# Attention of the last three batches on four 64x64 quadrants of the array

## The chip, the cores and the metric

The kernel runs on one core of one Trainium2 chip. A core has five engines that work side by side: TensorE (PE in the profile, its weight loads PEld), VectorE (DVE), ScalarE (ACT), GpSimd (POOL) and SyncE (SP). PE multiplies a stationary operand, loaded ahead as weights, with a moving operand, and writes the result to PSUM. Its array has 128 rows and 128 columns; a matmul whose operands cover 64 rows and 64 columns uses one quadrant of it. The row half follows from the SBUF partitions of the operands (0 to 63 or 64 to 127), the column half from the PSUM partitions of the output. DMA transfers are issued by POOL (loads that convert float32 to bfloat16) and by SP (transposes between SBUF tiles, and the stores).

The metric is device time in microseconds, the median of several runs; less is better.

## The reference

Two stages. The first is attention with 8 batches, 8 heads, 576 tokens and head size 64. The lower four heads see a plain window of 32 tokens, the upper four a dilated one: 32 tokens, every fourth. The second is a feed-forward block with a squared ReLU, on 4608 tokens of 512 features and a hidden size of 2048.

```python
scores = scale * np.matmul(q, k.transpose(0, 1, 3, 2))
mask_plain = (rel >= 0) & (rel < window)
mask_dil = (rel >= 0) & (rel < window * dilation) & (rel % dilation == 0)
scores = np.where(masks[None, :, :, :], scores, -1000000000.0)
attn = np.exp(scores - np.max(scores, axis=-1, keepdims=True))
attn = attn / (np.sum(attn, axis=-1, keepdims=True) + 1e-09)
out = np.matmul(attn, v)
x = out.transpose(0, 2, 1, 3).reshape(B * S, H * D)
h = np.maximum(x @ w_in, 0.0)
result = h * h @ w_out
```

## The kernel before, in words

**Feed-forward.** Tokens come in tiles of 512 (the first 1024 tokens in tiles of 256). A tile of 512 is 32 groups of four matmuls of 512 columns: 16 groups of `mm1` (L683), each followed by a ReLU on ACT (L696) and a square on DVE (L697), and 16 groups of `g2` (L725); after every fourth of these, ACT copies the result out (L731) and SP stores it. Four PSUM buffers `pf` rotate. Groups are numbered through the kernel; group 128 starts tile 4.

**Attention.** Heads go in pairs `e` = 0 to 3; head 2e lies in partitions 0 to 63, head 2e+1 in 64 to 127. Pairs 0 and 1 are plain, 2 and 3 dilated; they are taken in the order 0, 2, 1, 3. Tokens stand by their residue modulo 4 (`r`, 4 of them) and then by `m` (144 of them). Keys come in nine blocks of 64. For a plain pair, block `i` meets 24 positions of each residue, so 96 queries; for a dilated one, a block of 64 positions of one residue meets 96 or 80 positions of the same residue. The ninth block, the remainder of 64 tokens, meets 64 queries.

For batches 1 to 7 a block's keys stand block-diagonally in `kbd` (128x128: one head's keys in each half, zeros elsewhere) and its values likewise in `vbd`, so that one matmul of the full array serves both heads. `scores` (L312, L318) makes half a pair at a time: matmuls into a PSUM buffer `pa`, Exp on ACT (L322), a mask product on DVE (L323). For batches from 3 on it also adds the overlapping parts of neighbouring blocks into `pm` (L332), so that the sums need to stream only 576 columns per pair and not one per block and query. `pv` (L422, L424) makes the products with the values in `po` and the sums, with a block of ones, in `pd`; then Ln and Exp(-x) on ACT (L426, L427) and a product on DVE (L437) write the normalised result into `xT`, which the feed-forward part reads. There are two `pa`, one `po` and one `pd`.

**Batch 0** has a path of its own (`first_step`). Its scores (L559) and some of its products (L597) use two diagonal quadrants of 64x64 at a time. Its transposes (L507) use column halves, and its warming matmuls (L477, `idle`) the whole array.

**Operands.** Q and K of a batch are loaded by POOL (`load_qk`, L161), transposed by SP into `xx` (`cross`, L216), and rearranged by DVE into `qT` and `kbd` (`halves`: L256 for Q, L260 for K of plain pairs, L267 and L273 for dilated ones), 16 copies for Q and 24 for K per batch. V is loaded by POOL (`load_v`: L178 plain, L191 dilated, L197 remainder); DVE spreads the dilated part into `vbd` (`spread_v`, L207).

**Order.** The schedule is written by hand. `PROGRAM` names what runs after each group up to 128: `5q0` is Q of pair 0 of batch 5, `4b3` the second half of the scores of pair 3 of batch 4, `4o1` and `4p1` the products of the first and the second half of pair 1, `L5:...` a load. Batches 5 to 7 follow from rules at the end of the kernel: for batch b, pair number x of the order gets its scores `a` and `b` at groups 32(b-1) + 8x - 2 and + 0, its products `o` and `p` at + 3 and + 6. Each engine takes its instructions in the order in which they are written; V of batch b is loaded from group 32(b-2) on, Q and K from 32(b-3) + 6, the transposes are written at 32(b-2) + 5.

Of the kernel before, what the change touches and what calls it, by code (L numbers as in the profile page):

```python
# [12 lines left out]
RES = 4  # L13
# [16 lines left out]
    "2k1h | 2q1 2k2 L3:x | | 2q2 2p0 L3:vwpdr 2a1 | | | 2b1 | 2o1 2a2 2v2 2q3 | | 2p1f | 2k3 | 2b2 2o2 | 2v3 | "  # L30
    "2a3 2p2f L4:q10123 | 2b3 2o3 | 3k1 | 2p3 | 3q1v L4:q00123 | 3k0l | | 3a1 3k0h | | 3k2l | 3o1 3q0a | 3k2h "
    "| | | 3a0 | 3b1 | 3q2 | | 3p1 L4:x L4:vwpdr | 3v2 | 3b0 | 3a2 3q3l 3o0 3q3h 3k3 | | | 3o2 3b2 | 4q1 | 3p0 "
    "3v3 | 3a3 | 3p2 4q2 4q0 | L5:q10123 3b3 4k0al | 3o3 4k0ah | 4k1 | | L5:q00123 3p3 4k2 4k3 4a0 L5:vwpdr | "
    "| | 4b0 | | 4q3 | | 4o0 | | | 4a2 4v2 | 4b2 | 4a3 L5:x 4a1 | 4o2 | | | 4p2 L6:q00123 4v3 | | 4b1 | | 4p0 "
    "| | 4p1 | 5q0 5k0 | 4b3 | | | | 4o1 | | 5k2 L6:q10123 4o3 | 5q2 5k1 | | 4p3 | 5q1 |"
)


# [25 lines left out]
def kernel(  # L64
# [9 lines left out]
    nc = tc.nc  # L74
# [21 lines left out]
    PARTED = (0, 1)  # L96
    STAGE = (0, 1, 0, 2, 2, 2, 0, 1)
    ADDED = 3
    RING = 4 * S
    KT = DM // P  # L100
    NF = DFF // P
# [35 lines left out]
    xx = [const.tile([P, 2, H * 2 * M], bf16, name=f"xx{i}") for i in range(2)]  # L137
    qx, kx = [[t[:, x, :].rearrange("p (h c m) -> p h c m", h=H, c=2) for t in xx] for x in range(2)]
    qk0 = xx[0][:, :, :].rearrange("p x (e r m) -> p x e r m", e=NE, r=RES)
    k8 = const.tile([P, NE // 2, 64], bf16, name="k8")  # L140
    idle = const.tile([P, 256], bf16, name="idle")
    kbd = const.tile([P, NE, NB, P], bf16, name="kbd")
    vbd = [const.tile([P, NE, NB, P], bf16, name=f"vbd{i}") for i in range(2)]

    mk_dram = nc.inline_tensor(_masks(), name="mask_patterns")

# [156 lines left out]
    def scores(b: int, e: int, part: int):  # L303
        ps = ps_a.tile([P, 512], f32, name="pa")
        if part == 0:
            pts[e] = p_pool.tile([P, NB * 96], bf16, name="pt")
        pt = pts[e]
        n = 0
        for i, r, m0, m1 in blocks(b, e, part):
# [40 lines left out]
    def pv(b: int, e: int, part: int, spare=None, name=""):  # L350
# [71 lines left out]
            nc.tensor.matmul(oo, vb[:, e, i, :], rh, start=(x == 0), stop=(x == len(mms) - 1), skip_group_check=True)  # L422
        for x, (dd, rh) in enumerate(dms):
            nc.tensor.matmul(dd, ones[:, :], rh, start=(x == 0), stop=(x == len(dms) - 1), skip_group_check=True)  # L424
        rec = r_pool.tile([P, 512], f32, name="rec")
        nc.scalar.activation(rec[:, 0:n], d[:, 0:n], ACT.Ln)  # L426
        nc.scalar.activation(rec[:, 0:n], rec[:, 0:n], ACT.Exp, scale=-1.0)  # L427
        t0 = b * S % RING
# [12 lines left out]
    def step(b: int, code: str):  # L441
# [19 lines left out]
        else:  # L461
            pv(b, e, part)

    first = {}
    held = []
    sides = [slice(64 * hl, 64 * hl + 64) for hl in range(2)]
# [14 lines left out]
    def first_step(code: str):  # L481
# [56 lines left out]
        elif what == "S":  # L538
# [2 lines left out]
                first["S", e, part] = pool.tile([P, 512], f32, name=nm)  # L541
            ps = first["S", e, part]
            if part == 0:
                pts[e] = p_pool.tile([P, NB * 96], bf16, name="pt")
            bl = blocks(0, e, part)
            y = 0
            for x, (i, r, q0, q1) in enumerate(bl):
# [62 lines left out]
        elif what == "D":  # L610
            dms = first.pop(("D", e, part))
            for x, (dd, rh) in enumerate(dms):
                nc.tensor.matmul(
                    dd, ones, rh, start=(x == 0 and y0 == 0), stop=(x == len(dms) - 1), skip_group_check=True
                )
        else:
            n = 512 if part == 0 else w
            if what == "L":
                first["X", e, part] = rec = r_pool.tile([P, 512], f32, name="rec")
                nc.scalar.activation(rec[:, 0:n], first["P", e, part][1][:, 0:n], ACT.Ln)  # L620
            elif what == "X":
                rec = first["X", e, part][:, 0:n]
                nc.scalar.activation(rec, rec, ACT.Exp, scale=-1.0)
            else:
                o, rec = first["P", e, part][0][:, 0:n], first.pop(("X", e, part))[:, 0:n]
                to = xT[:, e, RES * m0 : RES * m0 + n]
                if part == 0:
                    to = xT[:, e : e + 2, 0:w]
                    o, rec = [x.rearrange("p (e n) -> p e n", e=2) for x in (o, rec)]
                nc.vector.tensor_tensor(out=to, in0=o, in1=rec, op=ALU.mult)  # L630
# [172 lines left out]
    def run(code):  # L803
# [21 lines left out]
        elif code[0] in "wW":  # L825
            n, _, at = code[1:].partition("+")
            turn(int(n), 512 if code[0] == "w" else 256, [int(x) for x in at])
        elif code[0] in "TCBSEPDXM" or code[0] == "L" and code[2:3] != ":":
            first_step(code)
        elif code[0] != "L":  # L830
            step(int(code[0]), code[1:])
        else:
            b, what, part, which = int(code[1]), code[3], code[4:5], code[5:]
            if what == "q":
                load_qk(b, None if part == "w" else int(part), [int(e) for e in which])
            elif what == "x":
                cross_all(b)
            elif what == "v":
                load_v(b, [0, 1] if part == "w" else [int(part)], which)
            else:  # L840
                (load_w_in if what == "i" else load_w_out)(int(part))
# [11 lines left out]
    head = groups[:G]  # L853
    groups[:NF] = [head[y] for y in (0, 1, 2, 3, 16, 4, 5, 17, 18, 19, 20, 21, 6, 7, 22, 23)]
    groups[NF:G] = [head[y] for y in (8, 9, 12, 13, 10, 11, 14, 15)] + head[24:32]
    for b in range(5, B):
        at = {"a": (-2, 8), "b": (0, 8), "o": (3, 8), "p": (6, 8), "v": (-4, 8)}
        at = {**({"k": (-9, 4), "q": (-9, 4)} if b > 5 else {}), **at}
        steps += attention_steps(b, G * (b - 1), at)

    steps += [(4 * G + 3, 5, "k3"), (4 * G + 3, 5, "q3")]
    steps.sort(key=lambda x: x[0])
    program = [x.split() for x in PROGRAM.split("|")]
    for code in program[0]:
        run(code)
    for g, group in enumerate(groups):
        for b in [x for x in CROSS if CROSS[x] == g]:
            cross_all(b)
        for b in [x for x in LOAD_V if LOAD_V[x] == g]:
            load_v(b, [0, 1])  # L870
        for b in [x for x in LOAD_QK if LOAD_QK[x] == g]:
            for part in range(2):
                load_qk(b, part, [0, 1, 2, 3])
# [1 line left out]
        for code in program[g + 1] if g + 1 < len(program) else ():  # L875
            run(code)
        while steps and steps[0][0] <= g:
            step(*steps.pop(0)[1:])


# [28 lines left out]
```

## Time and profile before

| What | Value |
|---|---|
| Runs before (median; lowest to highest) | 308.2 us; 307.83 to 308.27 us |
| Profiled execution: its span | 308.3 us |
| ReLU L696 on ACT | 144 of 599 ns |
| Square L697 on DVE | 144 of 422 ns |
| Ln L426, 128x288 on ACT | 23 of 411 ns |
| Exp L427, 128x288 on ACT | 24 of 443 ns |
| Product L437, 128x288 on DVE | 23 of 456 ns |
| K copy L260, 64x288 on DVE | 36 of 471 ns |
| Q copy L256, 64x288 on DVE | 84 of 258 ns |

The span is that of the same execution as all other rows; it lies 0.1 us over the median. Durations are those of one instruction from its start to its end; neighbours on an engine can overlap a little, and matmuls overlap a great deal, so their spacing is read from starts and not from durations. The last three batches run from about 152 to 249 us; from 249.5 us on only the feed-forward part is left. In that stretch the windows of one batch each have these busy times in us, with the number of instructions behind each:

| Window, us | PE | DVE | ACT |
|---|---|---|---|
| 154.5 to 186.2 | 31.70 (x234) | 23.89 (x84) | 20.76 (x45) |
| 186.2 to 218.0 | 31.80 (x235) | 24.24 (x87) | 20.86 (x46) |
| 218.0 to 249.6 | 31.60 (x230) | 19.25 (x66) | 20.66 (x45) |

### The profile page before, as it was taken

The numbers are of one execution on the slowest core, as the hardware profiler recorded it, in microseconds if no ns is written. First come the engines' busy times: TensorE is split into PE (matmuls) and PEld (weight loads), VectorE is DVE, ScalarE is ACT, GpSimd is POOL, SyncE is SP. The second block draws the span as 40 slices with busy tenths as digits, with TensorE's granted clock in tenths as the row PEclk, the third lists the DMA queues.
The fourth block names the chain that finished last, engine by engine and source line by source line (L and its number), as shares of the span: only waits on it lengthen the run. The fifth ranks groups of instructions, "written<-read, shape, count | busy, mean of one in ns | idle before, by whom it ended". The sixth has DMA issues, their size and how long they took to land.

```text
span 308.3 us, 6632 instructions
## 1 busy us (share of the span) xinstructions
PE 300.6 (97%) x2471; PEld 178.7 (58%) x2471; DVE 197.4 (64%) x649; ACT 199.1 (65%) x427; POOL 93.9 (30%) x138
## 2 busy tenths in 40 slices
PE   8988999999999999999999999999999999999995
PEld 3578846968855555555555555555555555445543
DVE  1565556998989889985798479946994334104400
ACT  6787748859878867784488448854786456216611
POOL 8479872496226245501541051000000000000000
PEclk9999999999999999999999999999999999999999
DMA  7999999999999959999799976401200210121012
GB/s 108 188 145 212 207 145 216 170 133 195 150 129 198 175 101 194 193 127 159 109 133 161 122 111 120 84 18 59 64 1 2 68 69 2 33 69 34 2 56 80
DMA packets 80287, 35.03 MB, mean 114 GB/s; under 512 B 49920, under 2 KB 75648, under 8 KB 80256
## 3 DMA queue, kind: packets, MB, share of 16 engines
q0 software_dynamic: 46592, 18.23, 54.6%
q1 hardware_dynamic: 32976, 16.06, 27.6%
q10 hardware_dynamic: 688, 0.33, 0.5%
q8 instruction: 19, 0.31, 0.4%
q14 instruction: 12, 0.10, 0.1%
HBM read 36.90 MB, written 9.44 MB: 150 GB/s over the span
## 4 chain that ended last, share of the span: by engine, by line
PE 89%; DMA 5%; POOL 2%; DVE 1%; issue 1%; ACT 0%; ACTq 0%; POOLq 0%
PE pf L683 39%; PE pf L725 39%; DMA w_in<-in_moe_w_in_dram 5%; PE po L422 3%; PE pd L424 2%; PE pa L312 2%; PE pa L318 1%; PE pa L236 1%; POOL vbd L178 1%; DVE qT L256 1%; POOL qb L161 1%; POOL kb L161 1%; PE pf L422 0%; POOL vd L184 0%; PE pf L424 0%
## 5 line engine op out<-in xcount | busy, mean ns | idle before, releaser
L683 PE MATMUL pf<-xT,w_in 128*128 128x512 bf16 (+1 forms) x704 | 133.0, 341 | 2.0 <-DMA w_in<-in_moe_w_in_dram 1.9
L725 PE MATMUL pf<-w_out_sb,h2T 128*128 128x512 bf16 (+2 forms) x592 | 134.3, 373 | 0.0
L683 PEld LDWEIGHTS <-w_in 128*128 128x128 bf16 x704 | 75.5, 113 | 42.2 <-DMA w_in<-in_moe_w_in_dram 2.5
L696 ACT ACTIVATE h2T<-pf 128x512 bf16<-128x512 f32 x144 | 83.8, 599 | 24.2 <-PE pf L683 23.5
L725 PEld LDWEIGHTS <-h2T 128*128 128x128 bf16 x592 | 53.8, 98 | 54.4
L697 DVE TENSOR_TENSOR h2T<-h2T 128x512 bf16<-128x512 bf16 x144 | 57.8, 422 | 38.8 <-ACT h2T L696 37.6
L731 ACT COPY osb<-pf 128x512 f32<-128x512 f32 (+1 forms) x36 | 20.7, 575 | 44.1 <-PE pf L725 40.2
L437 DVE TENSOR_TENSOR xT<-po,rec 128x288 bf16<-128x288 f32 (+2 forms) x51 | 23.2, 454 | 30.6 <-ACT rec L427 30.2
L178 POOL DMA_DIRECT2D vbd<-in_v_dram x36 | 25.8, 742 | 50.8 <-PE pd L424 22.8
L426 ACT ACTIVATE rec<-pd 128x288 f32<-128x288 f32 (+2 forms) x51 | 20.9, 411 | 20.6 <-PE pd L424 20.6
L322 ACT ACTIVATE pt<-pa 128x352 bf16<-128x352 f32 (+6 forms) x56 | 27.6, 499 | 6.3 <-PE pa L312 3.5
L427 ACT ACTIVATE rec<-rec 128x288 f32<-128x288 f32 (+2 forms) x56 | 24.8, 443 | 1.8
L422 PEld LDWEIGHTS <-vbd 128*128 128x128 bf16 x286 | 17.0, 97 | 10.3 <-issue 0.4
L256 DVE COPY qT<-xx 64x288 bf16<-64x288 bf16 x84 | 21.7, 258 | 1.1
L161 POOL DMA_DIRECT2D qb<-in_q_dram x18 | 13.1, 730 | 21.2 <-issue 10.1
L191 POOL DMA_DIRECT2D vd<-in_v_dram x24 | 14.7, 630 | 10.3 <-DMA kb<-in_k_dram 5.8
L422 PE MATMUL po<-pt,vbd 128*128 128x32 bf16 (+3 forms) x256 | 17.5, 198 | 0.1
L260 DVE COPY kbd<-xx 64x288 bf16<-64x288 bf16 x36 | 16.9, 471 | 0.5
L424 PE MATMUL pd<-pt,mk 128*128 128x96 bf16 (+6 forms) x138 | 15.5, 203 | 0.0
L161 POOL DMA_DIRECT2D kb<-in_k_dram x18 | 12.9, 719 | 0.5 <-DMA vd<-in_v_dram 0.5
L312 PE MATMUL pa<-qT,kbd 128*128 128x96 bf16 (+2 forms) x144 | 12.2, 202 | 0.0
L207 DVE COPY vbd<-vd 64x512 bf16<-64x512 bf16 (+1 forms) x38 | 11.1, 291 | 1.6 <-DMA vd<-in_v_dram 0.9
(100 smaller groups left out, 241.3 us busy)
## 6 DMA issues: line engine op xcount, KB each, us to landing
qb<-in_q_dram POOLq DMA_DIRECT2D x7, 320.0 KB, 7.3
kb<-in_k_dram POOLq DMA_DIRECT2D x7, 320.0 KB, 9.2
vd<-in_v_dram POOLq DMA_DIRECT2D x32, 64.0 KB, 5.3
w_in<-in_moe_w_in_dram POOLq DMA_DIRECT2D x4, 512.0 KB, 8.2
w_out_sb<-in_moe_w_out_dram POOLq DMA_DIRECT2D x4, 512.0 KB, 12.9
out_dram<-osb SPq DMA_DIRECT2D x16, 128.0 KB, 3.1
qb<-in_q_dram POOLq DMA_DIRECT2D x7, 256.0 KB, 7.6
kb<-in_k_dram POOLq DMA_DIRECT2D x7, 256.0 KB, 8.9
```

What stands on the lines that cost most here:

```text
L161: nc.gpsimd.dma_start(t[0:n, part, hs, :], src[b, hs, t0 : t0 + RES * n, :].rearrange("h (p r) d -> p h (r d)", r=RES))
L178: nc.gpsimd.dma_start(dst[rows, e, i0:i1, rows], v[b, 2 * e + hl, 64 * i0 : 64 * i1, :].rearrange("(i p) d -> p i d", p=64),)
L256: copy(qT[rows, e, :, m0 : m0 + n].rearrange("p (c j) m -> p j c m", j=2)[:, jj, :, :], src)
L322: nc.scalar.activation(pt[:, off : off + n], ps[:, 0:n], ACT.Exp, scale=SCALE)
L422: nc.tensor.matmul(oo, vb[:, e, i, :], rh, start=(x == 0), stop=(x == len(mms) - 1), skip_group_check=True)
L424: nc.tensor.matmul(dd, ones[:, :], rh, start=(x == 0), stop=(x == len(dms) - 1), skip_group_check=True)
L427: nc.scalar.activation(rec[:, 0:n], rec[:, 0:n], ACT.Exp, scale=-1.0)
L437: nc.vector.tensor_tensor(out=tok, in0=o if o is o3 else o[:, 0:n], in1=rec if o is o3 else rec[:, 0:n], op=ALU.mult)
L683: nc.tensor.matmul(to, w_in_sb[piece][:, kt, c0 : c0 + 509 : 4], rhs, start=(kt == kts[0] and x == 0), stop=(kt == kts[-1] and x == per - ...
L696: nc.scalar.activation(hv, acc[u][:, :].rearrange("p (x n) -> p x n", x=per), ACT.Relu)
L697: nc.vector.tensor_tensor(out=hv, in0=hv, in1=hv, op=ALU.mult)
L725: nc.tensor.matmul(cur[m][:, c0:c1], h2[:, f, P * m : P * m + P], w_out_sb[:, f, c0:c1], start=(f == 0), stop=(f == NF - 1),)
```

## The change

The change touches batches 5 to 7 alone (and where batch 4's last steps stand). Their block-diagonal operands go. Keys and queries of plain pairs are rearranged into `k_both` and `q_both`, in which the four plain heads stand in both partition halves, so that even blocks are read from the lower and odd blocks from the upper half; dilated pairs read keys and queries straight from `xx`. `v_rows` holds V as plain rows of 64. All of these lie in the memory of `kbd`, `qT` and `vbd`; the small tiles `k8` and `idle` move into `kbd`.

A new function, `quadrants`, writes one bundle of matmuls of 64x64: the products and sums of one pair (`pv`), then the scores of the next one (`sc`). For the scores, the row half `g` takes a key block (or a residue), the column half `c` the head: four quadrants. For the products, the values use the diagonal quadrants (g, g), the sums the other two (g, 1-g). Scores go to the two `pa`, one for each row half; the sums of overlapping blocks are no longer added beforehand (`pm` is gone), so a pair's sums stream as many columns as its values, in fewer and longer matmuls. The last 64 queries' results use the tails of the two `pa`.

Per batch there are now four bundles, 8 groups apart, at groups 32(b-1) - 4 + 8x. Exp and mask of a pair follow 2 and 3 groups later (`E`), the Ln 8 later, in the same place as the next bundle (`L`: four instructions, two of 64x64 and two of 64x512, which also move the sums to the other partition half), and Exp and product 9 later (`X`: one Exp of 128x576 and three products). In place of 40 copies for Q and K there are four for K of 64x1152 (`K`), four for Q of 64x1152 (`Q`) and four small ones for the remainder of dilated heads (`R`), written 15 to 5 groups ahead of group 32(b-1) + 0. `load_v_rows` makes ten transfers in place of ten: dilated first, then remainder, then plain. In `PROGRAM` the Q and K steps of batch 5 are gone, and `4b3`, `4o1`, `4o3` and `4p3` stand at groups 116, 120, 122 and 125 in place of 117, 121, 123 and 126.

```diff
-    "... L5:q00123 3p3 4k2 4k3 4a0 L5:vwpdr | "
+    "... L5:q00123 3p3 4k2 4k3 4a0 L5:V | "
-    "| | 4p1 | 5q0 5k0 | 4b3 | | | | 4o1 | | 5k2 L6:q10123 4o3 | 5q2 5k1 | | 4p3 | 5q1 |"
+    "| | 4p1 | 4b3 | | | | 4o1 | | L6:q10123 4o3 | | | 4p3 | |"
...
-    k8 = const.tile([P, NE // 2, 64], bf16, name="k8")
-    idle = const.tile([P, 256], bf16, name="idle")
     kbd = const.tile([P, NE, NB, P], bf16, name="kbd")
+    k8 = kbd[:, 3, 6, :].rearrange("p (e t) -> p e t", t=64)
+    idle = kbd[:, 3, 7:9, :].rearrange("p x t -> p (x t)")
+    v_rows = [t[:, 0:2, :, :].rearrange("p e i c -> p (e i c)").rearrange("p (e i d) -> p e i d", e=NE, d=D) for t in vbd]
+    q_both = qT[:, :, :, :]
+    k_both = kbd[:, 0:2, :, :].rearrange("p e i c -> p (e i c)").rearrange("p (h t) -> p h t", h=NE)
+    last = kbd[0:64, 2, 0:4, :].rearrange("p x c -> p (x c)").rearrange("p (x h t) -> p x h t", x=2, t=64)
...
+    def arrange(b: int, what: str, g: int, jj: int):
+        src, rows = sides[jj], sides[g]
+        n = H // 2
+        if what == "Q":
+            nc.vector.tensor_copy(q_both[rows, :, jj::2, :], qx[b % 2][src, 0:n, :, :])
+        elif what == "K":
+            nc.vector.tensor_copy(
+                k_both[rows, :, :].rearrange("p h (m c j) -> p j h c m", c=2, j=2)[:, jj, :, :, :],
+                kx[b % 2][src, 0:n, :, :],
+            )
...
+    def quadrants(sc=None, pv=None):
+        ps = [ps_a.tile([P, 512], f32, name="pa") for _ in range(2)]
...
+            o, d = ps_o.tile([P, 512], f32, name="po"), ps_d.tile([P, 512], f32, name="pd")
...
+            def value(rows_of, rhs, main=None, tail=None):
+                for g, rows in enumerate(sides):
+                    out, bank = (o4[main], "o") if tail is None else (tails[g][tail], "t")
+                    mm(out, g, g, rows_of(g, rows), rhs[rows], bank)
+
+            def total(rhs, main=None, tail=None):
+                for g, rows in enumerate(sides):
+                    out, bank = (main, "d") if tail is None else (tails[g][tail], "t")
+                    mm(out, g, 1 - g, ones[rows, 64 * g : 64 * g + 64], rhs[rows], bank)
...
+                for x, n in ((0, 4), (1, 3)):
+                    to = d4[:, :, 16 * x : 16 * x + 32 * n].rearrange("p r (i m) -> p i r m", m=32)
+                    total(wide(x, n), to[:, :, :, 0:24])
+                    for i in range(x, 2 * n, 2):
+                        value(lambda g, rows: vr[rows, e, i, :], blk(i), np.s_[:, :, 16 * i : 16 * i + 24])
...
+                for x, m0, m1, y in ((0, 0, 96, 0), (1, 64, 128, 96), (1, 128, M, 160)):
+                    w = m1 - m0
+                    for r in range(RES):
+                        if r < 2:
+                            rhs = pt2[r][:, :, y : y + w]
...
+            for z in range(4):
+                for g, rows in enumerate(sides):
+                    for c in range(2):
...
+                        mm(out, g, c, lhs, rhs)
+            for c in range(2):
...
...
-    for b in range(5, B):
-        at = {"a": (-2, 8), "b": (0, 8), "o": (3, 8), "p": (6, 8), "v": (-4, 8)}
-        at = {**({"k": (-9, 4), "q": (-9, 4)} if b > 5 else {}), **at}
-        steps += attention_steps(b, G * (b - 1), at)
-    steps += [(4 * G + 3, 5, "k3"), (4 * G + 3, 5, "q3")]
-    steps.sort(key=lambda x: x[0])
+    for b in range(NATURAL, B):
+        base = G * (b - 1) - 4
+        steps += [(base + y, b, f"K{x}") for y, x in ((-11, "00"), (-10, "01"), (-9, "10"), (-8, "11"))]
+        steps += [(base + y, b, f"Q{x}") for y, x in ((-6, "00"), (-5, "01"), (-4, "10"), (-3, "11"))]
+        steps += [(base + y, b, f"R{x}") for y, x in ((-2, "00"), (-1, "01"))]
+        for x, e in enumerate(ORDER):
+            at = base + 8 * x
+            steps.append((at, b, f"{'S' if b == NATURAL and x == 0 else 'B'}{e}"))
+            steps += [(at + 2, b, f"E{e}0"), (at + 3, b, f"E{e}1"), (at + 8, b, f"L{e}"), (at + 9, b, f"X{e}")]
+    steps.append((G * (B - 1) - 4, B - 1, f"P{ORDER[-1]}"))
+    steps.sort(key=lambda x: (x[0], x[2][0] in "LX"))
```

## The prediction

> **What bounds the kernel now.** I read the page first: busy shares and the chain of work that ended last.
>
> ```profile
> span 308.3 us, 6632 instructions
> PE 300.6 (97%) x2471; PEld 178.7 (58%) x2471; DVE 197.4 (64%) x649; ACT 199.1 (65%) x427; POOL 93.9 (30%) x138
> PEclk9999999999999999999999999999999999999999
> PE 89%; DMA 5%; POOL 2%; DVE 1%; issue 1%; ACT 0%; ACTq 0%; POOLq 0%
> ```
>
> PE is the chain for 89% of the span at full granted clock. So I took the chain in order of time, where each piece is start, length, what.
>
> ```profile
> 153.70 0.18 PE pa L312 x4
> ...
> 185.40 0.18 PE pa L312 x4
> ...
> 217.10 0.18 PE pa L312 x4
> ...
> 249.67 13.81 PE pf L683 x64
> 263.49 13.81 PE pf L725 x64
> ```
>
> The first three rows are the same scores of batches 5, 6 and 7: 31.70 us apart. Between two of them lie 32 groups of the feed-forward part (128 matmuls of 512 columns). The last two rows show these alone: 13.81 us per 64, so 27.62 per 32 groups. The attention of one batch therefore costs PE 31.70 - 27.62 = 4.08 us, and three cost **12.2 us**. The windows of these stretches show PE busy for all of 154.58 to 249.51: nothing else ends a wait there, and each us that PE saves or loses in these bundles is one of the span, as long as the other engines still deliver in time.
>
> **What a matmul costs.** The 512-wide ones start 13.81/64 = 215.8 ns apart, the 128-wide ones of the last group 55.7 ns: 0.417 ns a column and 2.4 ns each. Check on before: a batch streams 2 x 2240 columns in plain and 2 x 2112 in dilated pairs, 8704 x 0.417 = 3.63, plus 106 matmuls x 2.4 ns = 0.25: 3.9 of the 4.08. So before pays almost nothing but columns, and no change of array shape. Shapes change only in the first 20 us, where batch 0 already uses two diagonal quadrants. Timeline there (start, us, engine, line, tile, rows*columns, shape, count):
>
> ```profile
> 10.94 0.39 PE L477 MATMUL po<-idle 128*128 128x512 bf16 x1
> 11.26 0.31 PE L559 MATMUL pf<-xx 64*64 64x64 bf16 x8
> ...
> 13.56 0.44 PE L597 MATMUL po<-pt,vd 64*64 64x64 bf16 x16
> 13.94 0.39 PE L613 MATMUL pd<-pt,mk 128*128 128x256 bf16 x2
> ...
> 20.18 0.65 PE L559 MATMUL pa<-xx 64*64 64x32 bf16 x24
> ```
>
> **Shape change:** the 512-wide matmul at 10.94 should be followed after 0.216, the quadrants start after 0.32: 0.10 lost. At the other end, L597's last matmul starts 0.193 (its length) before 14.00, so at 13.81, should be followed after 0.03, and is after 0.13: 0.10 again. **Quadrants:** 24 matmuls from 20.18 to 20.83 carry 960 columns per quadrant (0.40 us) in 0.65 - 0.19 = 0.46 between first and last start: the two quadrants run side by side. Record by record a step of 96 columns takes 42.5 ns for both, the second starting 3.5 ns after the first; one of 64 columns with new weights (L597) takes 31.7.
>
> **The change, PE.** Per plain pair the scores are 4 rounds of 96 and one of 64: 4 x 42.5 + 32 = 0.202 us if all four quadrants run side by side; dilated 2 x 42.5 + 2 x 35.8 + 32 = 0.189. Products of a plain pair: values fill a diagonal quadrant with 7 x 96, 64, 32 and 64 columns, 7 x 42.5 + 3 x 32 = 0.394, sums the other diagonal with the same 832 columns; 0.40 with the starts 3.5 ns apart. Dilated: the sum for r=1 waits for that of r=0 in its quadrant (192 columns, 83 ns), and as PE issues in order, the values behind it wait too. The block of 96 columns then takes 0.177 to the next block's start, that of 64 0.138, that of 16 0.128, the remainder 0.06: 0.505. Twelve pairs: 6 x (0.202 + 0.189 + 0.40 + 0.505) = **7.8 us**. Bundles: 13 (S, 11 B, P), each with 0.10 in and 0.10 out: 13 x 0.194 = **2.5 us**. Sum 10.3 against 12.2: **1.9 us gained**.
>
> The trace has no four quadrants at once. The bounds: if side by side fully, 7.8; if the two column neighbours of one row group (same partitions, other moving data) take turns, every sum, value and score of a row group is in line: scores 0.43 and 0.405, products 0.78 and 0.83, 6 x 2.45 = 14.7. I take 7.8, by the nearest rows: L507's pairs, in one row group and two column halves, start 3.5 ns apart and step by 31.7 ns.
>
> [...]
>
> **The change, ACT and DVE.** Rows by form:
>
> ```profile
> L522 DVE COPY xx<-pa 128x320 bf16<-128x320 bf16 x2 | 0.9, 486 | 0.0
> L522 DVE COPY xx<-pa 128x256 bf16<-128x256 bf16 x2 | 0.8, 424 | 3.1 <-ACT xx L521 3.1
> L207 DVE COPY vbd<-vd 64x512 bf16<-64x512 bf16 x24 | 7.2, 300 | 0.4
> L630 DVE TENSOR_TENSOR xT<-po,rec 128x512 bf16<-128x512 f32 x1 | 0.7, 691 | 0.5 <-ACT rec L623 0.5
> L620 ACT ACTIVATE rec<-pd 128x512 f32<-128x512 f32 x1 | 0.6, 578 | 0.0
> ```
>
> The K copies (64x1152, written 4 elements apart) are like L522's: (486 - 424)/64 = 0.97 ns an element, 0.486 + 832 x 0.97 = 1.29 us each (bounds: 0.45, if as fast as a contiguous one, and 1.41 by L260's slope). Q copies are contiguous: L207's 300 and L267's 235 for 256 give 0.25 ns an element, 0.45 (bounds 0.45 and 1.29). Per batch the rows of 186 to 218 have 13.8 us of Q and K copies, spreads and adds; after it 4 K (5.2), 4 Q (1.8), the remainders (about 1.0) and 0.9 more in the products, so DVE is freed of 4.9 us, but what it has left comes in long pieces.
>
> Where that bites: **batch 4's last products**. DVE in before ends 4p0's product at 142.5. After it now stand K00 and K01 (to 145.1), 4p1's product (145.6), K10 (146.9), 4b3's mask and add (147.4), K11 (148.7), Q00 and Q01 (149.6), 4o1's product (150.0). 4o3, now in group 122, needs po and pd, which that product frees; group 122 ends at 149.42. PE stands **0.55 us** (0 with fast copies, 1.05 with 1.41), and all of the feed-forward part queues behind. Later batches: from about 173.2 (squares of the first half done) DVE has a mask, 4 K (5.2), a product (1.1), two masks (0.7) and 4 Q (1.8), 9.2 us, so 182.4; the bundle after group 156 starts at 183.19. Hidden, with 0.8 to spare; without it, the bundle waits.
>
> ACT: two Ln of 64x512 (0.58) and two of 64x64 (about 0.24 by the slope of L426) instead of two of 0.41: 0.8 us more per pair, less 0.2 at the Exp. In a stretch with evictions that makes 8 x 0.6 + 3.2 = 8.0 us of durations in 7.5 us, but ACT overlaps neighbours by 0.1 (L427 to the next), so 16 instructions fit: 0. The end of a batch: 4 Ln (1.35 overlapped), Exp 0.68, product 0.69, handovers 0.25: 3.0 us after the products; the next group that reads it comes 3 groups and 3 matmuls later, 3.2. I take 0, up to 0.3 at three places.
>
> Loads: ten V DMAs per batch before and after, same bytes; V of 6 now waits on POOL for 4p1 instead of 4p3, thus earlier. Q and K loads and the transposes on SP stay put; K00 of batch 5 at 142.5 comes after the last K transpose's packets (142). 0. Moving idle and k8 into kbd: 0, their readers end 60 us before kbd is zeroed.
>
> **Sum:** -1.9 + 0.55 = -1.35 us, against a span of 308.3, which lies 0.1 over the median 308.2: **306.8**. A measurement here can tell about 0.2%, 0.6 us, from no change.
>
> **Rivals.**
> 1. *Sums hold the values back* (14%): if matmuls must end in order, a 96-wide value behind a 384-wide sum starts 120 ns late, behind a 192-wide one 40. Products cost 0.164 (plain) and 0.055 (dilated) more, x 6 each: 1.3 us, **308.1**, no change. For it: no row mixes lengths. Against: the two quadrants of a pair end 3.5 ns apart without holding the next one. [...]
> 2. *Column neighbours take turns* (23%, slower): 14.7 + 2.5 + 0.55 = 17.7 against 12.2, **313.7**; partly (a round of four at 1.3 of its time: 7.8 to 10.2) 309.2. It turns the sign once a bundle's own time passes (12.2 - 2.5 - 0.55)/13 = 0.70 us. For it: the two moving streams read the same 64 partitions, and L507 has one and the same moving operand. Against: L507's weights differ and load side by side.
> 3. *DVE is late* (11%, slower): Q copies at 1.29 too: 1.7 more before 4o3, and 3.4 - 0.8 = 2.6 before the first bundle of batches 6 and 7: +6.9, **313.8**. Against: L256's 288 contiguous elements take 0.24 us.
>
> **Chances.** Forecast 52%, own range 305.8 to 307.6: with no stall 306.3, less something for shape changes hidden by waits; with 0.5 more stall and 0.3 at an end 307.6. To leave out no more than two in ten, the range reaches over rival 1 and the partial turns with a stall of 2 us more, and stops short of both full rivals at 313.7: **305.7 to 311.5**. Faster 0.51, same 0.14 (rival 1 and rims), slower 0.35.
>
> **What would show it.** Rounds of four 96-wide quadrant matmuls 42 ns apart with starts 3.5 ns apart (turns: 85). Values starting beside their sum, not after it. 0.1 us around each bundle. PE's spacing of batches near 27.6 + 4 x (0.6 to 0.7 + 0.2) = 31.0. K copies at 1.3 us, and idle before 4o3 released by DVE. The forecast is wrong if bundles exceed 0.7 us or if PE waits more than 1.9 us for DVE or ACT.

## The result, and the profile after

| | Before | After |
|---|---|---|
| Median of nine runs each | 308.12 us | 310.19 us |
| Lowest and highest | 306.96 and 308.33 us | 308.44 and 311.11 us |
| Profiled execution: span, and its time | 308.3 us | 309.3 us, 311.11 us |

The ratio is 1.0064, with a 95% interval of 1.0038 to 1.009: the change makes the kernel slower by 0.64%, where the forecast was 1.4 us faster. A run's time lies 1.7 to 1.9 us above its span wherever both are known (311.11 against 309.3). So before's profiled execution, with a span of 308.3, took some 310.1 us by this estimate, about 2 us over before's median; the 0.1 us ahead of the prediction compares a span with a time. The profiled execution of the changed kernel is the highest of its nine, and in four of the nine the mean granted clock is 0.992 to 0.994, in the others 0.999 or 1.0; these four are the four highest (310.55 to 311.11), so what the profile shows of a lost clock is in under half of the runs.

The page of the changed kernel: span, busy times, the granted clock in 40 slices, the chain's shares.

```profile
span 309.3 us, 7139 instructions
...
PE 300.2 (97%) x2795; PEld 174.5 (56%) x2795; DVE 190.5 (62%) x535; ACT 203.8 (66%) x439; POOL 97.9 (32%) x138
...
PEclk9999999999999999999799999999999999999999
...
PE 83%; DMA 10%; DVE 4%; POOL 1%; issue 1%; ACT 1%; DVEq 0%; ACTq 0%; POOLq 0%
```

PE's busy time is the same as before (300.2 against 300.6) and DVE's is 6.9 us less, as planned. But the chain has lost six points of PE to DMA and DVE, and one slice (the 20th, 147 to 155 us) has a granted clock of 7 tenths. The chain in order of time (start, length, what) shows the place:

```profile
125.78 15.51 DMA xx<-kb
141.47 1.38 issue
142.85 1.55 DVE kbd L500
...
151.23 2.77 PE pf L923 x8
...
250.67 13.81 PE pf L881 x64
264.49 13.81 PE pf L923 x64
```

From 125.8 to 150.4 us the chain is not PE's: it runs through the transposes of batch 5's keys and the K copies of L500. The last two rows answer those of before (L683 and L725 there): alone, 64 matmuls take 13.81 us as they did. DVE's timeline there (start, length, line, tiles, count, and in brackets the idle time before and what ended it):

```profile
139.61 0.49 DVE L444 TENSOR_TENSOR xT<-po,rec 128x320 bf16<-128x320 f32 x1 [1.39 <-ACT rec L434]
141.38 3.01 DVE L500 COPY kbd<-xx 64x1152 bf16<-64x1152 bf16 x2 [1.27 <-DMA xx<-kb]
144.43 0.49 DVE L444 TENSOR_TENSOR xT<-po,rec 128x320 bf16<-128x320 f32 x1
144.95 1.65 DVE L500 COPY kbd<-xx 64x1152 bf16<-64x1152 bf16 x1
...
147.22 1.44 DVE L500 COPY kbd<-xx 64x1152 bf16<-64x1152 bf16 x1
148.69 1.29 DVE L498 COPY qT<-xx 64x1152 bf16<-64x1152 bf16 x2
150.00 0.42 DVE L444 TENSOR_TENSOR xT<-po,rec 128x256 bf16<-128x256 f32 x1
```

DVE waits 1.27 us for the transposes, makes four K copies and two Q copies, and only then writes the product of 4o1 (150.00), which frees `po` and `pd`. In before, DVE had been idle for 1.50 us when it came to that product, and PE went into 4o3 (there L422) without a wait. DVE's row and PE's, of before:

```profile
149.62 0.42 DVE L437 TENSOR_TENSOR xT<-po,rec 128x256 bf16<-128x256 f32 x1 [1.50 <-ACT rec L427]
```

```profile
148.56 1.89 PE L725 MATMUL pf<-w_out_sb,h2T 128*128 128x512 bf16 x8
150.28 0.34 PE L422 MATMUL po<-pt,vbd 128*128 128x96 bf16 x5
```

Of the changed kernel, PE's timeline, and the windows (length, busy us of each engine with instructions, clock, DMA share, GB/s) of the wait and of what follows:

```profile
145.30 1.89 PE L923 MATMUL pf<-w_out_sb,h2T 128*128 128x512 bf16 x8
150.48 0.48 PE L429 MATMUL po<-pt,vbd 128*128 128x96 bf16 x5 [3.29 <-DVE xT L444]
...
151.07 2.94 PE L923 MATMUL pf<-w_out_sb,h2T 128*128 128x512 bf16 x8
```

```profile
149.00:150.40 1.40, 0.00 (x0) 0.00 (x0) 1.34 (x3) 0.00 (x0) 1.40 (x3) 0.79 0.80 51
150.40:151.00 0.60, 0.52 (x8) 0.52 (x8) 0.54 (x3) 0.00 (x0) 0.60 (x1) 0.50 1.32 84
...
153.00:153.50 0.50, 0.50 (x3) 0.23 (x2) 0.39 (x2) 0.50 (x1) 0.00 (x0) 0.79 1.39 182
```

4o3 (L429) starts 3.46 us later than PE could have started it (3.29 idle, and what the last matmul overlaps). From 149.8 to 153.2 the granted clock is half: the row with 0.50, and the mixed rows on both sides (0.79 over 1.40 us is 0.59 us at half). The eight 512-wide matmuls from 151.07 on start up to 0.427 apart in place of 0.216. That costs 1.3 us more: from the start of 4o3 to the first bundle it is 3.45 us, and 2.15 in run 9 below, which has the same order and the full clock.

The bundles themselves are as forecast. PE's timeline of one with plain products and dilated scores, and of the matmuls around it:

```profile
161.07 0.59 PE L881 MATMUL pf<-xT,w_in 128*128 128x512 bf16 x2
161.59 0.35 PE L530 MATMUL pd<-pt,mk 64*64 64x384 bf16 x2
161.60 0.36 PE L530 MATMUL po<-pt,vbd 64*64 64x96 bf16 x8
...
162.00 0.34 PE L530 MATMUL pa<-xx 64*64 64x96 bf16 x16
...
162.30 0.62 PE L881 MATMUL pf<-xT,w_in 128*128 128x512 bf16 x2
```

The values (96 wide, second L530 row) start 0.01 us after the 384-wide sums that stand ahead of them, not after their end; from 161.59 to the next L881 at 162.30 lie 0.71 us. Counted between the neighbours of 512 columns, beyond their spacing, this kind takes PE 0.795 us, the other kind (dilated products, plain scores) 0.870.

To see the loss and the gain apart, the two profiles are laid beside each other by the start of a group of the feed-forward part, and the time from there to group 283 is compared (after less before): from group 112 on +3.40 us, from 120 +3.40, from 124 -1.10, from 128 -1.61, from 192 -0.70. So all that comes behind group 124 gains 1.1 to 1.6 us, and 4.5 us are lost between groups 120 and 124, where nothing but 4o3 stands still (3.46 and 1.3 us of half clock, the last 0.25 of which falls behind group 124).

### The profile page after: what moved, and what is told of

Its sections match the earlier page's. It is cut to its first block, busy times and chain, and to the rows that moved or that the text cites. A ratio compares the mean times of both kernels' runs of the same rounds, so it can differ in the third digit from the quotient of the medians.

```text
span 309.3 us, 7139 instructions
## 1 busy us (share of the span) xinstructions
PE 300.2 (97%) x2795; PEld 174.5 (56%) x2795; DVE 190.5 (62%) x535; ACT 203.8 (66%) x439; POOL 97.9 (32%) x138
## 4 chain that ended last, share of the span: by engine, by line
PE 83%; DMA 10%; DVE 4%; POOL 1%; issue 1%; ACT 1%; DVEq 0%; ACTq 0%; POOLq 0%
PE pf L881 37%; PE pf L923 36%; DMA xx<-kb 5%; DMA w_in<-in_moe_w_in_dram 2%; DMA kb<-in_k_dram 2%; DVE kbd L500 2%; PE po L429 1%; PE pa L530 1%; PE pd L431 1%; PE pa L243 1%; PE pa L319 1%; PE pd L530 1%; DVE qT L263 1%; PE po L530 1%; POOL qb L168 1%
## 5 line engine op out<-in xcount | busy, mean ns | idle before, releaser
L881 PE MATMUL pf<-xT,w_in 128*128 128x512 bf16 (+1 forms) x704 | 131.3, 341 | 0.6 <-DMA w_in<-in_moe_w_in_dram 0.6
L881 PEld LDWEIGHTS <-w_in 128*128 128x128 bf16 x704 | 76.5, 114 | 43.6 <-DMA w_in<-in_moe_w_in_dram 0.9
L433 ACT ACTIVATE rec<-pd 128x288 f32<-128x288 f32 (+2 forms) x27 | 11.1, 410 | 13.6 <-PE pd L431 13.6
L500 DVE COPY kbd<-xx 64x1152 bf16<-64x1152 bf16 x12 | 17.7, 1475 | 1.5 <-DMA xx<-kb 1.3
L329 ACT ACTIVATE pt<-pa 128x352 bf16<-128x352 f32 (+6 forms) x32 | 15.8, 504 | 4.1 <-PE pa L319 2.9
L657 ACT ACTIVATE pt<-pa 128x448 bf16<-128x448 f32 (+3 forms) x24 | 12.2, 509 | 9.1 <-DVE xT L648 9.1
L444 DVE TENSOR_TENSOR xT<-po,rec 128x288 bf16<-128x288 f32 (+2 forms) x27 | 12.3, 454 | 9.3 <-ACT rec L434 8.9
L646 DVE TENSOR_TENSOR xT<-po,rec 128x512 bf16<-128x512 f32 x12 | 8.3, 692 | 14.0 <-ACT rec L643 13.1
L434 ACT ACTIVATE rec<-rec 128x288 f32<-128x288 f32 (+2 forms) x32 | 14.2, 443 | 1.0
L429 PEld LDWEIGHTS <-vbd 128*128 128x128 bf16 x166 | 9.6, 98 | 8.4 <-issue 4.0
L639 ACT ACTIVATE rec<-pd 64x512 f32<-64x512 f32 x24 | 13.9, 579 | 0.0
L429 PE MATMUL po<-pt,vbd 128*128 128x96 bf16 (+3 forms) x136 | 9.4, 200 | 3.5 <-DVE xT L444 3.5
L486 POOL DMA_DIRECT2D vbd<-in_v_dram x12 | 11.9, 1001 | 0.2 <-issue 0.2
```

Source lines behind the costliest of these rows:

```text
L329: nc.scalar.activation(pt[:, off : off + n], ps[:, 0:n], ACT.Exp, scale=SCALE)
L500: nc.vector.tensor_copy(k_both[rows, :, :].rearrange("p h (m c j) -> p j h c m", c=2, j=2)[:, jj, :, :, :], kx[b % 2][src, 0:n, :, :],)
L639: nc.scalar.activation(rec[to, 0:512], d[at, :], ACT.Ln)
L881: nc.tensor.matmul(to, w_in_sb[piece][:, kt, c0 : c0 + 509 : 4], rhs, start=(kt == kts[0] and x == 0), stop=(kt == kts[-1] and x == per - ...
```

## The experiments

The theory, A: the bundles gain what was forecast, and what DVE has queued ahead of batch 4's last products, the K copies above all, gives it back. Its rivals: the bundles gain nothing (B); the late landing of the transposes alone is at fault (C). Whether POOL's earlier loads have a part in it is asked by run 4.

| Run | Median (lowest to highest), us | Ratio to before (95%) |
|---|---|---|
| changed kernel | 310.19 (308.44 to 311.11) | 1.0064 (1.0038 to 1.009) |
| K of one pair on ACT | 311.02 (309.53 to 313.77) | 1.0115 (1.0058 to 1.0172) |
| 4o3 in a tile of the ring | 308.46 (307.05 to 312.0) | 1.0033 (1.0002 to 1.0063) |
| K two groups later | 311.49 (310.46 to 313.61) | 1.0129 (1.0082 to 1.0176) |
| V loads of batch 6 held | 311.87 (310.97 to 312.68) | 1.0132 (1.0099 to 1.0165) |
| new order, first | 308.45 (308.05 to 309.13) | 1.0006 (0.9992 to 1.0021) |
| new order, K earlier | 309.86 (309.09 to 310.21) | 1.0051 (1.0032 to 1.0071) |
| same, bundles split | 311.96 (311.22 to 312.39) | 1.0118 (1.0096 to 1.0141) |
| new order, second | 307.17 (306.31 to 308.07) | 0.9955 (0.9933 to 0.9978) |
| changed kernel, short K | 307.13 (306.03 to 309.06) | 0.997 (0.9946 to 0.9995) |

**1. Two of batch 5's K copies on ACT.**

```diff
-            arrange(b, what, e, int(code[2]))
+            arrange(b, what, e, int(code[2]), nc.scalar.copy if b == 5 and what == "K" and e == 1 else nc.vector.tensor_copy)
```

> Edit: two of batch 5's four K copies (K10, K11) run on ACT instead of DVE; nothing else moves. Theory A (DVE's queue at the hand-over from batch 4 to batch 5 is the loss): DVE is freed of 3.1 us (1.65 + 1.44) ahead of 4o1's product, so that product ends near 146.8 in the clock of the changed kernel's profile instead of 150.4, the 3.46 us that PE stands before 4o3 become 0 to 0.3, no slow matmuls of 0.43 us follow it, and the time is about 1.3 us under the kernel before (306.8). Rival B (the bundles or other engines are the loss, DVE only happens to be last): the time stays within 0.5 us of 310. Rival C (the transposes' landing alone holds K00, and ACT now waits for it as well): PE still stands 1 to 2 us there, 308.5.

ACT's timeline, then DVE's:

```profile
143.31 2.76 ACT L500 COPY kbd<-xx 64x1152 bf16<-64x1152 bf16 x1
146.10 0.46 ACT L329 ACTIVATE pt<-pa 128x352 bf16<-128x352 f32 x1
146.59 2.76 ACT L500 COPY kbd<-xx 64x1152 bf16<-64x1152 bf16 x1
...
149.85 0.39 ACT L433 ACTIVATE rec<-pd 128x256 f32<-128x256 f32 x1
```

```profile
150.72 0.42 DVE L444 TENSOR_TENSOR xT<-po,rec 128x256 bf16<-128x256 f32 x1 [2.71 <-ACT rec L434]
```

On ACT the copy takes 2.76 us, on DVE 1.45. The Exp of 4b3 (L329) and the Ln of 4o1 (L433) queue behind the two, and DVE waits 2.71 us for them: 4o1's product comes at 150.72 again, and PE stands 2.69 us. The wait kept its place and changed its cause, and the time is 4.2 us over what A said (306.8). The run does not speak against A, but says nothing for its price.

**2. 4o3 in a tile of the feed-forward part's ring**, so that it need not wait for 4o1's product.

```diff
-    "| | 4p1 | 4b3 | | | | 4o1 | | L6:q10123 4o3 | | | 4p3 | |"
+    "| | 4p1 | 4b3 | | | | 4o1 | | L6:q10123 4o3f | | | 4p3 | |"
```

> Edit: batch 4's products 4o3 go to two feed-forward PSUM buffers instead of po and pd, so that they need not wait for 4o1's product; DVE's queue is as in the changed kernel. Theory A (DVE is late as a whole): the wait before 4o3 goes, but the first bundle (S0) now waits for the last Q copy, which ends near 151.5 against 149.3 for the bundle: about 2.2 us of stall there, below the 3.46 of the changed kernel, the slow matmuls after it fewer or none; time about 308 to 308.5. Rival D (the single po and pd are the cause): no stall anywhere, 306.8. Rival B: 310, unchanged.

PE's timeline:

```profile
148.08 0.34 PE L429 MATMUL pf<-pt,vbd 128*128 128x96 bf16 x5
...
150.23 0.23 PE L530 MATMUL pa<-qT,kbd 64*64 64x96 bf16 x2
151.61 0.36 PE L530 MATMUL pa<-qT,kbd 64*64 64x96 bf16 x16 [1.15 <-DVE qT L498]
```

The wait ahead of 4o3 is gone, and the ratio falls from 1.0064 to 1.0033, to where A had it (308 to 308.5 us). DVE is as late as before, though: its last Q copies are the next to be waited for, inside the first bundle, which takes 1.76 us in place of 0.41. The clock stays at 1.0 in this profile.

**3. Batch 5's K copies two groups later.**

```diff
-        steps += [(base + y, b, f"K{x}") for y, x in ((-11, "00"), (-10, "01"), (-9, "10"), (-8, "11"))]
+        steps += [(base + y + 2 * (b == 5), b, f"K{x}") for y, x in ((-11, "00"), (-10, "01"), (-9, "10"), (-8, "11"))]
```

> Edit: batch 5's four K copies are written two groups later (115 to 118), so that 4p1's product stands before them on DVE. Theory A with the landing as one part: the 1.3 us in which DVE waited for the K transposes now holds 4p1's product (0.5 us); 4o1's product stands behind the same 6 us of copies, and ends about 0.5 to 1 us earlier: PE stands 2 to 3 us before 4o3 instead of 3.46; time 309 to 310. Rival C (the wait for the transposes is the whole loss): the stall falls by its 1.3 us and the order of the copies is all that matters, 308 or less.

No wait for the transposes is left (the K copies start at 143.57, behind 4p1's product), and PE still stands 3.14 us ahead of 4o3. C, the landing alone, falls. The time is worse than A said, for the clock; the windows:

```profile
151.40:155.00 3.60, 3.30 (x15) 1.60 (x16) 2.25 (x8) 1.44 (x3) 2.92 (x5) 0.50 1.21 111
...
157.00:158.00 1.00, 1.00 (x13) 0.60 (x12) 0.00 (x0) 0.00 (x0) 0.00 (x0) 0.77 1.26 157
```

It is half until about 157.5, so what PE does in the 6 us from 151.5 on would take 3 us at full clock: 3 us lost on top of the wait.

**4. POOL waits for 4o3's product before it loads V of batch 6** (a copy of two elements that reads it).

```diff
         for b in [x for x in LOAD_V if LOAD_V[x] == g]:
+            if b == 6:
+                nc.gpsimd.tensor_copy(hold[:, :], xT[0:1, 3, 0:2])
             load_v_rows(b)
```

> Edit: POOL waits for 4o3's product of batch 4 before it issues the V loads of batch 6 (and the Q and K loads of batch 7 behind them), by one copy of two elements that reads that product. In the changed kernel POOL issues ten loads from 137 to 150 us, while DVE makes the long copies. Theory E (POOL's descriptor writing slows DVE's copies): K10, 1.65 us, and Q00 and Q01, 0.53 and 0.72, fall to the 1.45 and 0.45 of batches 6 and 7; 0.5 to 0.7 us off the stall, 0.3 to 0.7 us off the time. If POOL has no part in it, the copies keep their lengths and the time stays. In both cases some 2.8 us or more of the stall stays, as theory A has it.

Groups of DVE by form, 140 to 152 us (busy us, mean ns, idle before), this kernel first, the changed one second:

```profile
L501 DVE COPY kbd<-xx 64x1152 bf16<-64x1152 bf16 x4 | 5.8, 1454 | 0.2 <-DMA xx<-kb 0.2
L499 DVE COPY qT<-xx 64x1152 bf16<-64x1152 bf16 x4 | 1.8, 456 | 0.1
```

```profile
L500 DVE COPY kbd<-xx 64x1152 bf16<-64x1152 bf16 x4 | 6.1, 1523 | 1.3 <-DMA xx<-kb 1.3
L498 DVE COPY qT<-xx 64x1152 bf16<-64x1152 bf16 x4 | 2.2, 552 | 0.1
```

With POOL silent, no copy is stretched, the wait for the transposes is 0.17, and PE stands 1.73 us ahead of 4o3 in place of 3.46 (2.8 or more were expected), with the clock at 1.0. The copies account for 0.63 of the difference, as expected (0.5 to 0.7 us), so the loads that now start earlier were not free. The other 1.1 us is the shorter wait for the transposes, and that it is POOL's doing is not shown: the transposes land at 141.4 us here and at 141.3 in the changed kernel's profile, and DVE reaches the K copies 1.2 us later (141.3 against 140.1). The time is nevertheless higher, against the expectation: the loads that were held back delay batch 6's transposes, DVE waits 2.47 us for these at 176, and the bundle behind, at 183, stands some 2.7 us in three pieces. It moves the wait to the next batch.

**5. A new order: 4o1, 4o3 and 4p3 ahead of the K and Q copies that they wait behind**, and bundles of batch 5 at groups 128, 135, 142 and 149.

```diff
-    "| | 4p1 | 4b3 | | | | 4o1 | | L6:q10123 4o3 | | | 4p3 | |"
+    "| | 4p1 | 4b3 | 4o1 | | | L6:q10123 4o3 | | 4p3 | |"
...
+    ats = [128, 135, 142, 149] + [G * (b - 1) - 4 + 8 * x for b in range(6, B) for x in range(NE)] + [G * (B - 1) - 4]
...
+        if b == NATURAL:
+            ks, qs, rs = [115, 117, 120, 122], [122, 122, 123, 123], [124, 125]
```

> Edit: only the places of the hand-over steps change. 4o1, 4o3 and 4p3 stand at groups 117, 120 and 122 instead of 120, 122 and 125; batch 5's K copies stand behind the products of batch 4 (after 4p1, 4o1, at 120 and after 4p3), its Q copies at 122 and 123, its remainders at 124 and 125; its bundles at 128, 135, 142 and 149 instead of 124, 132, 140 and 148. No instruction is added or dropped. Theory A (the bundles gain what was forecast, and DVE's queue ahead of 4o1's product gives it back): no PE wait above 0.5 us from group 112 on, no matmuls of 0.43 us, time 306.6 (1.3 us under the kernel before). Rival B (the quadrant bundles themselves are the loss): 309 to 310. Rival F (copies and loads collide wherever they stand): a wait of 1 to 3 us appears before the first bundle at group 128 instead, 308.

It is 1.7 us below the changed kernel's median, level with before, and 1.8 above what A said (306.6). Nothing waits ahead of 4o3. What is left, in PE's timeline:

```profile
153.76 0.36 PE L530 MATMUL pa<-qT,kbd 64*64 64x96 bf16 x16 [0.32 <-DVE qT L498]
...
181.80 0.27 PE L530 MATMUL pd<-pt,mk 64*64 64x192 bf16 x2 [0.59 <-DVE pt L659]
...
182.77 0.36 PE L530 MATMUL pa<-qT,kbd 64*64 64x96 bf16 x16 [0.33 <-DVE qT L498]
```

The first bundle waits 0.52 for Q, and the first of batch 6 takes 2.28 us with 1.4 of waiting: for a mask (`pt`) and for Q. The masks of the bundle at 142 now come two groups later and push batch 6's K and Q copies back.

**6. As 5, and the first K copy of batches 6 and 7 four groups earlier. 7. As 6, and every bundle split into products and, one group later, scores.**

```diff
-        ks, qs, rs = [base + y for y in (-11, -10, -9, -8)], [base + y for y in (-6, -5, -4, -3)], [base - 2, base - 1]
+        ks, qs, rs = [base + y for y in (-15, -11, -10, -9)], [base + y for y in (-6, -5, -4, -3)], [base - 2, base - 1]
```

```diff
-            quadrants(sc=(b, e), pv=(b, ORDER[at - 1]) if at else (b - 1, ORDER[-1]))
+            quadrants(pv=(b, ORDER[at - 1]) if at else (b - 1, ORDER[-1]))
+        elif what == "C":
+            at = ORDER.index(e)
+            quadrants(sc=(b, e), ps=op[(b, ORDER[at - 1]) if at else (b - 1, ORDER[-1])][2])
...
+            if not (b == NATURAL and x == 0):
+                steps.append((at + 1, b, f"C{e}"))
```

In these two the earlier copy overwrites `k_both` while batch 5's pair 1 has yet to be scored, so that pair is scored partly against batch 6's keys.

> Edit: as e7_handover, and the first K copy of batches 6 and 7 four groups earlier (group 141 and 173 instead of 145 and 177), into DVE's idle time before the last squares. Theory A: the dilated bundles at 156 and 188, which wait for the last Q copy in the changed kernel (1.00 us instead of 0.87), lose that wait: 0.25 to 0.3 us less than e7_handover; 306.3. If the wait has another cause, same as e7_handover.

> Edit: as e8_handover_k, but each of the 11 bundles of products and scores is split: products where they were, scores one group later, so that the array changes its shape 22 times more. Theory: each change costs 0.095 us, the first matmuls after it 0.01 to 0.03 more, and the join of products and scores no longer overlaps (0.02 us): 11 x 0.21 to 0.25 = 2.3 to 2.8 us over e8_handover_k. If the changes of shape hide behind loading weights or the queue, less than 1 us.

Run 6 was to gain 0.25 to 0.3 us on run 5, and lost 1.4. Its waits for Q did go (the bundles take 0.910 and 0.871). But PE's timeline shows the scores of pair 1 of batch 5, which are written behind the copy, waiting for it:

```profile
169.35 0.39 PE L530 MATMUL pa<-qT,kbd 64*64 64x96 bf16 x18 [1.50 <-DVE kbd L500]
```

Run 7 costs 2.1 us more than run 6 (311.96 against 309.86; 2.3 to 2.8 were expected) for 11 splits, 0.19 each. The two pieces of a bundle, in PE's timeline:

```profile
161.22 0.35 PE L530 MATMUL pd<-pt,mk 64*64 64x384 bf16 x2
...
161.74 1.05 PE L884 MATMUL pf<-xT,w_in 128*128 128x512 bf16 x4
162.72 0.54 PE L530 MATMUL pa<-xx 64*64 64x96 bf16 x15
```

Products and sums alone take 0.610 (plain) or 0.672 (dilated), scores 0.54 to 0.60, together 0.35 to 0.41 more than in one bundle. Some 0.18 of that is a wait behind the first score; what is left is the 0.2 us of one shape change in and one out, the price that the forecast had put on a bundle. Eleven times 0.35 to 0.41 would be some 4.2 us, and the end moved by half of that, chiefly because the split also takes away a wait that run 6 had: its bundle with the scores of pair 1 took 2.56 us in place of 0.87, and in run 7 these scores stand a group later, start at 170.24, behind the end of the copy (168.74 and 1.45), and wait 0.15 at most. Another 0.36 us of run 6, a wait for a square at 205.6, is gone in run 7 too.

**8. The second new order**: as 5, but Q copies one group later, so behind 4p3's product, and the bundles at 128, 134, 140 and 148, so that the masks come ahead of batch 6's K copies.

```diff
-    "| | 4p1 | 4b3 | 4o1 | | | L6:q10123 4o3 | | 4p3 | |"
+    "| | 4p1 | 4b3 | 4o1 | | | L6:q10123 4o3 | | | 4p3 | |"
...
-    ats = [128, 135, 142, 149] + [G * (b - 1) - 4 + 8 * x for b in range(6, B) for x in range(NE)] + [G * (B - 1) - 4]
+    ats = [128, 134, 140, 148] + [G * (b - 1) - 4 + 8 * x for b in range(6, B) for x in range(NE)] + [G * (B - 1) - 4]
...
-            ks, qs, rs = [115, 117, 120, 122], [122, 122, 123, 123], [124, 125]
+            ks, qs, rs = [115, 117, 119, 121], [123, 123, 124, 124], [128, 129]
```

> Edit: as e7_handover, but 4p3 one group later (123), batch 5's K copies at 115, 117, 119 and 121, Q at 123 and 124, remainders at 128 and 129, and its bundles at 128, 134, 140 and 148, so that the masks before batch 6's K copies and the bundle at 156 stand as far apart as in the changed kernel. In e7_handover PE waited 0.52 us for Q before the bundle at 128 and 1.4 us for Q before that at 156. Theory A: both waits go to 0 to 0.3 us, and the time falls by 1.3 to 1.9 us below e7_handover, to 306.6 to 307.1, under the kernel before. Rival B (the quadrant bundles do not gain): not under the kernel before.

**307.17 us, ratio 0.9955 (0.9933 to 0.9978): faster than before, and than the changed kernel,** whose ratio, from other runs of before, has an interval that lies wholly above. It is 0.07 us above where A put it (306.6 to 307.1); by the medians of the two (307.17 against 307.99) the gain on before is 0.8 us. The page of this kernel, and the windows where the changed one stood still:

```profile
span 305.5 us, 7139 instructions
...
PEclk9999999999999999999999999999999999999999
```

```profile
144.00:148.00 4.00, 4.00 (x28) 1.99 (x27) 3.90 (x6) 1.81 (x4) 4.00 (x4) 1.00 1.34 176
148.00:152.00 4.00, 4.00 (x28) 1.99 (x27) 3.65 (x6) 1.34 (x3) 4.00 (x6) 1.00 0.84 119
```

PE is busy throughout (4.00 of 4.00) at full clock, with DVE as loaded as ever (3.90 and 3.65): the same work in another order. From group 112 on it is 1.03 us shorter than before. One bundle still waits 0.34 for Q.

**9. The changed kernel's own order, with batch 5's K copies moving one head of four**: the same instructions in the same places, shorter. The kernel leaves out the keys of the other three plain heads in each copy.

```diff
         elif what == "K":
+            n = 1 if b == NATURAL else n
...
-                k_both[rows, :, :].rearrange("p h (m c j) -> p j h c m", c=2, j=2)[:, jj, :, :, :],
+                k_both[rows, 0:n, :].rearrange("p h (m c j) -> p j h c m", c=2, j=2)[:, jj, :, :, :],
```

> Edit: the changed kernel, with its own order, but batch 5's four K copies move one head of the four (a quarter of the elements; the other three plain head pairs of batch 5 are scored against what stood there). It takes 3.3 us of copying away from DVE, and nothing else. Theory A: no stall before 4o3 beyond 0.3 us, none before the first bundle, no matmuls of 0.43 us: 306.6 to 306.9, and the spread between runs falls to that of the kernel before. Rival C (the wait for the transposes is what counts): K00 waits as before, PE still stands 1 us or more: 308.

DVE's timeline, and the first window again:

```profile
142.86 0.98 DVE L501 COPY kbd<-xx 64x288 bf16<-64x288 bf16 x2 [0.59 <-DMA xx<-kb]
...
148.52 0.42 DVE L444 TENSOR_TENSOR xT<-po,rec 128x256 bf16<-128x256 f32 x1 [0.68 <-ACT rec L434]
```

```profile
144.00:148.00 4.00, 4.00 (x26) 1.99 (x25) 3.67 (x7) 1.33 (x3) 4.00 (x7) 1.00 1.19 141
```

The copies wait 0.59 us for the transposes, and POOL issues its loads as early as in the changed kernel, and yet PE never stands: 4o1's product now waits for ACT, not for DVE. The bundles sum to the same 10.47 us. From group 112 on it is 1.36 us shorter than before; the time of 307.13 us is 0.2 over what A said (306.6 to 306.9). That shows A: DVE's K-copy time ahead of 4o1's product decides. B falls, since these bundles gain. C falls by run 3, where no wait for the transposes was left and PE stood 3.14 us; here 0.59 of its 1.27 us is still there. POOL's loads alone fall, since they are still there and stretch the first two Q copies as before (0.53 and 0.73 us). The runs spread from 306.03 to 309.06; that the spread would vanish with the stall was not borne out.

## Why the prediction was wrong

**Right, with their numbers.** Four quadrants run side by side: the starts of a round lie 3 to 16 ns apart, and a round of 96 columns mostly takes 42 to 43 ns with new weights each time, some 67 for the first one of a bundle. Shape change: 93 to 98 ns, forecast 0.10. The 13 bundles sum to 10.47 us against a forecast of 10.3; without the 0.13 us that each of two of them waits for Q, it is 10.2. Q copy 0.45, Ln 0.58 and 0.22, Exp 0.68, product 0.69: all as costed.

**Both PE rivals fall.** Sums do not hold the values back (values start 3 to 7 ns behind the 384-wide sums ahead of them; whether they also end before these stays open, since ends are modelled), and column neighbours do not take turns (rounds of 42 to 43 ns, not 85).

**The step that failed is "PE stands 0.55 us (0 with fast copies, 1.05 with 1.41)"** before 4o3. It measured 3.46 us, and the half clock that follows took 1.3 more. Run 4 helps to split the 3.46: there it is 1.73, and the other 1.73 is 1.1 us of waiting for the transposes (1.27 less 0.17, not shown to be POOL's), 0.3 of K copies (6.1 less 5.8) and 0.33 of Q00 and Q01 (1.25 less 0.92). So the sign of being wrong that the prediction named, over 1.9 us of waiting for DVE, came true. That 310.19 lies inside its range of 305.7 to 311.5 is in part luck: the range was stretched over two rivals that did not happen, and the direction was wrong.

- *The K copy* was priced at 1.29 us from L522, a copy out of PSUM with up to 320 elements, carried to 1152; it takes 1.45, above the upper bound of 1.41. L260's own two rows out of PSUM (337 ns for 160 elements, 482 for 288) give 1.13 ns an element, and so 1.45 from its 471 ns. Four copies: +0.64.
- *"K00 of batch 5 ... comes after the last K transpose's packets (142). 0."* In before the transfer lands at 142.8, 0.3 us behind that point already. In the changed kernel's profile DVE gets there 2.4 us earlier, at 140.1; the transfer was issued 2.7 us earlier and took 15.5 us in place of 14.3, so it lands at 141.3: 1.27 us of waiting (0.44 in run 2, 0.17 in run 4). The 2.4 us need not be the change's doing: before's feed-forward part had waited for `w_in` until 26.41 us, that of run 9, in the changed kernel's order, until 26.17, that of the changed kernel's profile began the same stretch at 23.97.
- *The V loads of batch 6, "thus earlier", at no cost.* POOL issues them from 137 to 150 us, and in that time K copies take up to 1.65 us in place of 1.45, Q copies 0.53 and 0.72 in place of 0.45; with POOL held (run 4), 1.454 and 0.456. So run 4 agrees that one slows the other, by 0.1 to 0.3 us a copy, where one POOL instruction takes 0.6 to 1.8 us; by what mechanism no run shows, and the writing of descriptors, of which the expectation of run 4 speaks, stands in no trace.
- *The clock* was in no term: a long wait was priced as its length alone.
- Of the 1.73 us of run 4, 0.55 was forecast, 0.64 is the K copies and 0.17 the transposes. The other 0.4 is mostly time between instructions that the sum had at nothing: in run 4 some 0.25 us between the pieces of DVE's queue (13 to 34 ns each) and 0.06 from 4o1's product to 4o3.

**"Hidden, with 0.8 to spare"** for batches 6 and 7 was too generous as well: the longer K copies (0.64 together) and the order took the 0.8, and the bundles there wait 0.13 us for Q each.

**The gain** was forecast at 1.9 us and is 1.36 where nothing stands still (run 9). Bundles of 10.47 against 12.2 leave 1.73; one wait of 0.16 us on `xT` at group 160 and 10 to 30 ns at the second matmul after each of 13 bundles come off that.

**Rival 3** had the engine and the place right and the price wrong: it took slow Q copies, with 1.7 us more before 4o3 and 2.6 before the first bundles of batches 6 and 7. The Q copies were fast; it was K, the landing and POOL, and almost only before 4o3.

## What to carry to other kernels

When many small copies become a few long ones, look past the sum: in an engine's queue, ask of each long piece which product or mask stands behind it, and whether another engine, through a buffer with no spare, stands still until that comes. Here DVE was freed of 7 us in all and lost 4.8 us of PE's time in one place; moving three steps ahead of the copies, with the bundles behind them set apart anew, gave it back (run 8), while giving the copies to another engine, a spare buffer, or holding another queue back each moved the wait to the next in line. Don't count on a transfer to the microsecond from one profile: from issue to landing this one took 14.3 us in before and 15.5 in the changed kernel.

## What the hardware showed

**A wait of 3 us costs a second time.** The windows put the fall of the granted clock at 149.8, 2.6 us into PE's idle time, and its return at 153.2: 3.4 us at half. In run 3 (2.97 us idle) it fell 2.1 us into the idle time, at 150.65 (mean 0.87 over 148.5 to 151.4), and came back at 157.46 (mean 0.77 over 157 to 158): 6.8 us, twice as long. Idle times of 2.53 (run 1), 1.56 (run 4) and 1.15 us (run 2) left it at 1.0. The length of the idle time alone does not set the moment: 2.1 us of it had been enough in run 3, and 2.53 were not in run 1. What sets it, no run shows. The records of the granted clock in the two profiles have full-clock stretches of 143.36 and 157.01 us (changed kernel, with the half-clock one of 3.41 between them) and of 300.37 us (before): 42, 46 and 88 times 3.413.

**The price of writing apart.** A copy of 64x1152 bf16 takes DVE 0.45 us when it writes adjacent elements and 1.45 when it writes every fourth, and ACT 2.76.

**POOL pays more than DVE.** The four loads of L486 that POOL issues beside these copies take 1.82, 1.57, 1.66 and 0.73 us in the changed kernel, and 0.78, 0.76, 0.84 and 0.82 in run 9, where the K copies take 0.48 to 0.78 us.
